# Decode attention plus MLP on one Trainium2 core: the second head's keys loaded in two halves, with a TensorE wait for the first half in round 0

## The chip, the core and the metric

The kernel runs on one core of one Trainium2 chip. The metric is the device time of one execution, in microseconds (us). Three runs of the kernel before the change took 1281.58, 1281.71 and 1282.12 us; their median is 1281.71 us. A difference of 0.2% is 2.6 us.

## The reference, cut to what matters

One token `x` (512 values) passes a layer norm, attends over a cache of 32768 positions in each of 32 heads, is projected and added back, and then passes a second layer norm and a small MLP with a mish activation.

```python
q = (layernorm(x) @ wq).reshape(B, 1, H, 128).transpose(0, 2, 1, 3)      # H = 32
scores = einsum("bhqd,bhkd->bhqk", q, k_cache) * 128 ** -0.5             # 32768 keys per head
o = einsum("bhqk,bhkd->bhqd", softmax(scores), v_cache)
h = x + o.transpose(0, 2, 1, 3).reshape(B, 1, 4096) @ wo
z = layernorm(h) @ w1 + b1
h2 = h + (z * tanh(softplus(z))) @ w2
```

All of it is bfloat16. The two caches are 8 MB per head each, 512 MB (537 million bytes) in all, and each byte is read once: the work is almost wholly the reading of the caches.

## The kernel before, in words

**Memory.** The caches pass through `ring`, six slots of 32 KB per partition (lines 321 to 323 and 354). A head's keys fill two slots: partition p holds the 256 keys 256p to 256p+255, so one partition's share of one head is one run of 64 KB in HBM. Keys of even heads live in slots 0 and 1, those of odd heads in slots 2 and 3, values in slots 4 and 5 (`slot_of`, line 461). `wq` starts in the slots of the values.

**The order of the loads** is one list (`order`, lines 446 to 449), which SyncE walks (lines 536 to 571) and which ends in one DMA queue: `wq`, the keys of head 0, the keys of head 1, the values of head 0, the keys of head 2, the values of head 1, and so on, then the weights of the tail. Before it starts a load, SyncE waits until the place is free (`freed_by`, line 481; for values line 565): the values of head 0 for the last use of `wq`, the keys of head 2 for the last transpose of head 0, the values of head 1 for the last product with the values of head 0. A load raises the semaphore `ready` of its slot. `pieces` (line 427) says which loads are cut: the keys of head 0 in two halves of 128 keys per partition, the values of the last head in six parts; every other one is a single DMA of 128 runs of 64 KB.

**TensorE's program** is a loop that exists once in the code and is run 32 times with the round in a register (`_pe_rounds`, line 170). Its parts lie in the code in this order: entry (with the 128 small products that make the queries, line 621), `top`, `head`, `skip`, `mid`, `tail`, `turn`, `rest`. Round n runs `head(n)`: 32 groups of 8 transposes of 128 keys (line 666), each group copied from PSUM to SBUF by VectorE (line 672) and, three groups later, multiplied by the query (line 642); then VectorE takes the maximum (line 706). At the start of `head` TensorE waits for the keys (`keys_in`, lines 76 to 80): both homes' `ready` semaphores against a value worked out from the round. After that come the softmax steps `soft_a` (line 712, maximum over the partitions), `soft_b` (line 717, spread of that maximum) and the exponential on ScalarE (line 722). In round 0 these are the separate block `turn` (lines 741 to 744), which is run once and jumps back to `top`. In every later round they are interleaved in `rest` (lines 746 to 756) with the 256 products with the values of the head before (`pv`, line 693), split 64, 64 and 128.

Of the kernel before, what the change touches and what calls it, by code (L numbers as in the profile page):

```python
# [291 lines left out]
def bass_sequential_preLN__mha_block_cached__dense_activation_mish__decode_kernel(  # L292
    nc: bass.Bass,
    A_x: bass.AP,
    A_k_cache: bass.AP,
    A_v_cache: bass.AP,
    A_wq: bass.AP,
    A_wo: bass.AP,
    B_x: bass.AP,
    B_w1: bass.AP,  # L300
    B_b1: bass.AP,
    B_w2: bass.AP,
    out: bass.AP,
):
    build_kernel(nc, A_x, A_k_cache, A_v_cache, A_wq, A_wo, B_w1, B_b1, B_w2, out)


def build_kernel(nc, A_x, A_k_cache, A_v_cache, A_wq, A_wo, B_w1, B_b1, B_w2, out):
# [3 lines left out]
    H = HD // Dh  # L312
# [29 lines left out]
    def sb(shape, dt, name):  # L342
        cm = nc.sbuf_tensor(name, shape, dt)
        t = cm.__enter__()
        allocs.append(cm)
        return t.ap()
# [21 lines left out]
    gmax = sb([1, 1], F32, "gmax")  # L368
# [39 lines left out]
    sem = nc.alloc_semaphore  # L408
# [3 lines left out]
    ready = [sem(f"ready{i}") for i in range(NS)]  # L412
# [12 lines left out]
    CUTS = {"k": [TPS], "v": [TPS // 2, TPS, 192, 224, 240]}  # L425

    def pieces(what):
        kind, h = what
        at = CUTS[kind] if what in (("k", 0), ("v", H - 1)) else []
        return list(zip([0] + at, at + [SCOLS]))  # L430

    def cut_at(kind, h, r):
        return r in [r0 for r0, _ in pieces((kind, h))]

    def uncut(what):


        kind, h = what
        for r in CUTS[kind]:
            if not cut_at(kind, h, r) and (h == 0 or cut_at(kind, h - 1, r)):  # L440
                n = 1
                while h + n < H and not cut_at(kind, h + n, r):
                    n += 1
                yield r, n
# [5 lines left out]
    cut_sems = {k: {r: sem(f"cut_{k}_{r}") for r in CUTS[k]} for k in CUTS}  # L450

    s_wl = sem("wl")
    w1_sems = [sem(f"w1_{n}") for n in range(len(W1P))]
    w2_sems = [sem(f"w2_{n}") for n in range(len(W2P))]

# [5 lines left out]
    def slot_of(what):  # L461
        if what in HOMES:
            return HOMES[what]
        if what[0] in ("w1", "w2"):
            return HOMES[WL]
        return V_HOME if what[0] == "v" else what[1] % 2 * HALVES
# [6 lines left out]
    def ready_wait(what):  # L473
        if what == WL:
            return (s_wl, 16)
        return (ready[slot_of(what)], 16 * fills[what])

    def free_name(what):
        return "free" + "_".join(map(str, what))

    def freed_by(what):
        if what == WO:
            return done_with("k", H - 2, 0, SCOLS)
        if what[0] == "k" and what[1] > 1:
            return done_with("k", what[1] - 2, 0, SCOLS)
        if what == ("v", 0):
            return [free_name(WQ)]
        return []

    def tiles_of(what):  # L490
        return ring[:, slot_of(what):slot_of(what) + HALVES, :].rearrange("p s (r d) -> p (s r) d", d=Dh)

    def keys_of(cache, h):
        return cache[0, h, :, :].rearrange("(p r) d -> p r d", r=SCOLS)
# [8 lines left out]
    def done_with(kind, h, r0, r1):  # L503
        if kind == "v":
            return [f"pv{h}_{r1}" if r1 in V_EVENTS else f"pv{h}"]
        return [free_name(("k", h, half)) for half in range(HALVES) if r0 < (half + 1) * TPS and r1 > half * TPS]
# [15 lines left out]
    def program(S):  # L522
# [3 lines left out]
        v = nc.vector  # L526
# [4 lines left out]
        def start(dst, src, s):  # L531
            S.dma(SP, lambda: sp.dma_start(dst, src).then_inc(s, 16))  # L532
# [3 lines left out]
        for what in order:  # L536
            slot = slot_of(what)
            if what == ("k", 1):
                S.stay(SP)
            S.wait(SP, freed_by(what))  # L540
            flat = ring[:, slot, :]
            if what[0] == "wq":
                S.wait(SP, ["b1z"])
                start(b1r[0:FJ, :], B_b1[0:FJ * 128].rearrange("(j p) -> j p", j=FJ), s_b1)
                start(b1r[FJ:FJ + 1, 0:FLAST], B_b1[FJ * 128:F].rearrange("(o p) -> o p", o=1), s_b1)
            elif what[0] == "wo":
                start(flat, A_wo.rearrange("(p j) n -> p (j n)", j=32), ready[slot])
            elif what == WL:
                start(wol_v, A_wo[(H - 1) * Dh:H * Dh, :], s_wl)
            elif what[0] == "w1":  # L550
                k = what[1]
                start(w1_v[:, k, :], B_w1[k * 128:(k + 1) * 128, :], w1_sems[k])
            elif what[0] == "w2":
                n = what[1]
                if n + 1 < len(W2_J):
                    j0, j1 = W2_J[n], W2_J[n + 1]
                    start(w2_v[:, j0:j1, :], B_w2[j0 * 128:j1 * 128, :].rearrange("(j p) n -> p j n", p=128), w2_sems[n])
                else:
                    start(w2_v[0:FLAST, FJ, :], B_w2[FJ * 128:F, :], w2_sems[n])
            else:  # L560
                kind, h = what
                rows = keys_of(A_k_cache if kind == "k" else A_v_cache, h)
                for r0, r1 in pieces(what):
                    if kind == "v" and h:
                        S.wait(SP, done_with(kind, h - 1, r0, r1))
                    start(tiles_of(what)[:, r0:r1, :], rows[:, r0:r1, :], cut_sems[kind][r0] if r0 else ready[slot])

                for r, n in uncut(what) if kind == "v" else [(r, H - 1) for r in CUTS["k"] if h == 2]:
                    S.dma(SP, lambda r=r, n=n: sp.sem_inc(cut_sems[kind][r], 16 * n))
        S.dma(SP, lambda: sp.dma_start(out[0, 0, :].rearrange("(c m) -> c m", c=KC), outr[0:128:32, :]).then_inc(s_out, 16),  # L570
              waits=["fin"])
# [20 lines left out]
        for c in range(2 * KC):  # L592
            cols = xr[0:1, c:D:KC] if c < KC else xr[0:1, (c - KC) * 128:(c - KC + 1) * 128]
            S.step(PE, lambda c=c, cols=cols: t_.matmul(X_REG[:, c:c + 1], cols, identb[0:1, 0:1], start=True, stop=True),
                   name=("xT" if c == 2 * KC - 1 else None), waits=(["identb", (s_x, 16)] if c == 0 else ()))
# [22 lines left out]
        for h in range(H):  # L618
            for kc in range(KC):
# [3 lines left out]
                       name=(["q", free_name(("wq",))] if last else None),  # L623
                       waits=(["xn0", ready_wait(("wq",))] if h == 0 and kc == 0 else ()))
# [90 lines left out]

        def soft_b(h):
            S.step(PE, lambda: t_.matmul(B_REG, onesm[0:1, :], gmax[:, :], start=True, stop=True),  # L717
                   name=f"B{h}", waits=[f"gmax{h}", "consts0"], kind="B")
            S.step(DVE, lambda: v.tensor_scalar_mul(nb[:, :], B_REG, -SC), name=f"nb{h}", waits=[f"B{h}"], kind="nb")  # L719

        def soft_exp(h):
# [19 lines left out]
        def turn():  # L741
            soft_a(0)
            soft_b(0)
            soft_exp(0)

        def rest(i):
            t = i - 1
            soft_c(t)
            pv(t, 0, TPS // 2)
            S.unless_final(PE, "soft_a", lambda: soft_a(i))  # L750
            pv(t, TPS // 2, TPS)
            S.unless_final(PE, "soft_b", lambda: soft_b(i))
            pv(t, TPS, SCOLS)
            oev(t)
            if t < H - 1:
                soft_exp(i)
# [84 lines left out]
    log = {}  # L841
    counted = _Sched(nc, False, events, sems, log)
    program(counted)
    nc.sync.dma_start(ring[:, slot_of(WQ), :], A_wq.rearrange("(p k) n -> p (k n)", k=KC)).then_inc(ready[slot_of(WQ)], 16)
    with nc.Block() as block:
        for eng_name, attr in ((POOL, "gpsimd"), (SP, "sync"), (DVE, "vector"), (ACT, "scalar"), (PE, "tensor")):
            emitter = _Sched(nc, True, events, sems, log, only=eng_name)

            def _run(eng, emitter=emitter):
                program(emitter)  # L850
            getattr(block, attr)(_run)
            assert emitter.cnt == counted.cnt
# [31 lines left out]
```

## Time and profile before

| | |
|---|---|
| median of three runs | 1281.71 us |
| the profiled execution's own time | 1281.4 us |
| its span, first to last instruction | 1279.6 us |
| what lies around the span | 1.8 us |
| bytes moved by DMA | 548.35 MB, mean 429 GB/s |
| TensorE matmuls busy | 1019.0 us (80%) |
| VectorE busy | 716.1 us (56%) |
| ScalarE, GpSimd busy | 20.8 us, 0.8 us |

TensorE's work is counted twice in the profile, as PE (matmuls) and PEld (weight loads, which lie beside the matmuls). "issue" is time in which an engine waited for nothing that the profile shows. SPq is SyncE's queue of DMA issues. The DMA queue named "instruction" carries the engines' own code. Times of the trace count from the first instruction of the span. The columns of the view of stretches are: the stretch, its length, then for each engine the busy time and the number of recorded instructions, the granted TensorE clock, the share of the 16 DMA engines that was busy, and GB/s. Register and branch instructions aren't recorded there. In the DMA views a packet is counted where it starts.

### The profile page before, as it was taken

What the parts mean: (1) busy time and instruction counts of PE and PEld (TensorE: products, weight loads), DVE (VectorE), ACT (ScalarE), POOL (GpSimd) and SP (SyncE); (2) the same over time, 40 slices, a digit from 0 to 9 for tenths busy, and PEclk for the clock granted to TensorE, in tenths of its full rate; (3) what the DMA queues carried; (4) which work ended last, traced back from release to release, by engine and by line L of the source; (5) the groups of instructions that cost most, each with busy time, mean ns of one, the idle gap of its engine ahead of it and who ended that gap; (6) DMA issues with size and microseconds to landing.
All of it is one profiled execution on the core that took longest, in us unless ns stands there. A gap on an engine that the chain in (4) does not pass through costs nothing.

```text
span 1279.6 us, 54437 instructions
## 1 busy us (share of the span) xinstructions
PE 1019.0 (80%) x25044; PEld 992.2 (78%) x25044; DVE 716.1 (56%) x1252; ACT 20.8 (2%) x71; POOL 0.8 (0%) x8
## 2 busy tenths in 40 slices
PE   3699777788777798777797777897777887777987
PEld 3699777788777798777797777897777887777885
DVE  2566654466654566545566544666445666445661
ACT  0000000000000000000000000000000000000000
POOL 0000000000000000000000000000000000000000
PEclk9888777788777788767788776888677887767885
DMA  9979999999999999999999999999999999999998
GB/s 425 420 339 426 445 440 426 426 426 459 426 426 426 449 436 426 426 426 459 426 426 426 453 432 426 426 434 451 426 426 426 457 428 426 426 436 449 426 426 355
DMA packets 12584, 548.35 MB, mean 429 GB/s; under 512 B 1343, under 2 KB 2848, under 8 KB 3616
## 3 DMA queue, kind: packets, MB, share of 16 engines
q1 hardware_dynamic: 12574, 548.22, 99.3%
q8 instruction: 8, 0.13, 0.0%
q10 hardware_dynamic: 2, 0.00, 0.0%
HBM read 548.21 MB, written 0.00 MB: 428 GB/s over the span
## 4 chain that ended last, share of the span: by engine, by line
DMA 55%; DVE 23%; PE 18%; SPq 2%; issue 2%; POOL 0%; POOLq 0%
DMA ring<-in_A_k_cache_dram 54%; DVE ering L672 23%; PE ops L693 9%; PE tps L666 7%; SPq L532 2%; PE sps L642 1%; PE hlp L717 1%; PE hlp L712 1%; DMA ring<-in_B_w_dram 1%; PE hlp L727 0%; PE tps L829 0%; DVE pmax L706 0%; DVE outr L834 0%; DVE gmax L714 0%; SPq L68 0%
## 5 line engine op out<-in xcount | busy, mean ns | idle before, releaser
L666 PE MATMUL tps<-identb,ring 128*128 128x128 bf16 x8192 | 671.1, 233 | 218.4 <-DMA ring<-in_A_k_cache_dram 214.5
L672 DVE COPY ering<-tps 128x1024 bf16<-128x1024 bf16 x1024 | 669.7, 692 | 274.5 <-PE tps L666 274.1
L666 PEld LDWEIGHTS tps<-identb,ring 128*128 x8192 | 524.3, 104 | 221.1 <-issue 221.1
L642 PE MATMUL sps<-qcur,ering 128*128 128x1 bf16 x8192 | 343.9, 164 | 11.3 <-DVE ering L672 6.6
L642 PEld LDWEIGHTS sps<-qcur,ering 128*128 128x128 bf16 x8192 | 309.9, 97 | 14.2 <-DVE ering L672 9.4
L693 PEld LDWEIGHTS ops<-pbuf,ring 128*128 128x128 bf16 x8192 | 226.4, 103 | 15.7 <-issue 12.4
L693 PE MATMUL ops<-pbuf,ring 128*128 128x1 bf16 x8192 | 231.1, 165 | 3.1 <-DMA ring<-in_A_v_cache_dram 2.5
L701 DVE TENSOR_TENSOR oT<-ops,rtotc 128x1 f32 x31 | 5.0, 161 | 107.8 <-PE ops L693 107.8
L714 DVE TENSOR_REDUCE gmax<-hlp 1x1 f32<-1x128 f32 x32 | 8.9, 278 | 63.4 <-PE hlp L712 63.4
L719 DVE TENSOR_SCALAR nbias<-hlp 128x1 f32<-128x1 f32 x32 | 5.1, 158 | 63.5 <-PE hlp L717 63.5
L722 ACT ACTIVATE pbuf<-sps,nbias 128x256 bf16<-128x256 f32 x32 | 15.2, 475 | 1229.4 <-PE ops L693 1171.7
L706 DVE TENSOR_REDUCE pmax<-sps 128x1 f32<-128x256 f32 x32 | 13.6, 425 | 14.3 <-PE sps L642 14.3
L712 PE MATMUL hlp<-ident,pmax 128*1 128x128 f32 x64 | 17.2, 365 | 3.5 <-issue 3.5
L717 PE MATMUL hlp<-gmax,onesmat 1*128 1x1 f32 x64 | 18.5, 356 | 0.4 <-DVE gmax L714 0.4
L717 PEld LDWEIGHTS hlp<-gmax,onesmat 1*128 1x128 f32 x64 | 15.8, 304 | 1.3 <-DVE gmax L714 0.9
L727 PE MATMUL hlp<-esum,onesmat 128*128 128x1 f32 x64 | 12.3, 261 | 5.3 <-issue 2.8
L727 PEld LDWEIGHTS hlp<-esum,onesmat 128*128 128x128 f32 x64 | 9.8, 192 | 7.9 <-issue 7.9
L621 PE MATMUL hlp<-xnT,ring 128*128 128x1 bf16 x128 | 3.5, 165 | 9.1 <-DMA ring<-in_A_wq_dram 9.1
L621 PEld LDWEIGHTS hlp<-xnT,ring 128*128 128x128 bf16 x128 | 3.5, 104 | 9.2 <-issue 9.2
L729 DVE RECIPROCAL rtotc<-hlp 128x1 f32<-128x1 f32 x32 | 5.4, 168 | 4.2 <-PE hlp L727 2.4
L625 DVE CAST qT<-hlp 128x32 bf16<-128x32 f32 x1 | 0.2, 192 | 11.4 <-PE hlp L621 11.4
L722 ACT ACTIVATION_READ_ACCUMULATOR pbuf<-sps,nbias 128x1 f32 x32 | 6.2, 194 | 0.0
(75 smaller groups left out, 37.9 us busy)
## 6 DMA issues: line engine op xcount, KB each, us to landing
ring<-in_A_k_cache_dram SPq DMA_DIRECT2D x2, 4096.0 KB, 26.6
ring<-in_A_v_cache_dram SPq DMA_DIRECT2D x3, 2048.0 KB, 11.3
ring<-in_A_wq_dram SPq DMA_DIRECT2D x1, 4096.0 KB, 12.1
ring<-in_A_wo_dram SPq DMA_DIRECT2D x1, 4096.0 KB, 35.3
ring<-in_B_w_dram SPq DMA_DIRECT2D x4, 344.0 KB, 16.8
ring<-in_A_v_cache_dram SPq DMA_DIRECT2D x1, 1024.0 KB, 14.3
ring<-in_A_v_cache_dram SPq DMA_DIRECT2D x2, 512.0 KB, 15.5
ring<-in_B_w_dram SPq DMA_DIRECT2D x1, 640.0 KB, 16.9
```

The source lines that it names most:

```text
L532: S.dma(SP, lambda: sp.dma_start(dst, src).then_inc(s, 16))
L621: S.step(PE, lambda h=h, kc=kc: t_.matmul(Q_REG[:, h:h + 1], wq_v[:, kc, h * Dh:(h + 1) * Dh], xnT[:, 0, kc:kc + 1], start=(kc == 0), stop ...
L642: S.step(PE, lambda r=r: t_.matmul(S_ps[:, col0 + r:col0 + r + 1], ering[:, bg % NE, r, :], qcur[:, :], start=True, stop=True), name=(name ...
L666: S.step(PE, lambda r=r, at=at: t_.matmul(tb[:, r * 128:(r + 1) * 128], key_tile(S, at), identb[:, :], is_transpose=True, start=True, stop ...
L672: S.step(DVE, lambda: v.tensor_copy(ering[:, bg % NE, :, :].rearrange("p r d -> p (r d)"), tb[:, :]), name=f"ev{bg}", waits=[f"trb{bg}"], ...
L693: S.step(PE, lambda r=r: t_.matmul(o_ps[:, 0:1], vt[:, r, :], pbuf[:, r:r + 1], start=(r == 0), stop=(r == SCOLS - 1)), name=(names or Non ...
L706: S.step(DVE, lambda: v.tensor_reduce(pmax[:, :], S_ps[:, 0:SCOLS], AXX, ALU.max), name=f"pmax{h}", waits=[f"qkh{h}"], kind="pmax")
L712: S.step(PE, lambda: t_.matmul(A_REG, pmax[:, :], ident[:, :], start=True, stop=True), name=f"A{h}", waits=[f"pmax{h}", "ident", f"rcp{h - ...
L714: S.step(DVE, lambda: v.tensor_reduce(gmax[:, :], A_REG, AXX, ALU.max), name=f"gmax{h}", waits=[f"A{h}"], kind="gmax")
L717: S.step(PE, lambda: t_.matmul(B_REG, onesm[0:1, :], gmax[:, :], start=True, stop=True), name=f"B{h}", waits=[f"gmax{h}", "consts0"], kind ...
L722: S.step(ACT, lambda: a.activation(pbuf[:, :], S_ps[:, 0:SCOLS], ACTF.Exp, bias=nb[:, :], scale=SC, accum_out=esum[:, :]), name=f"exp{h}", ...
L727: S.step(PE, lambda: t_.matmul(C_REG, onesm[:, :], esum[:, :], start=True, stop=True), name=f"C{h}", waits=[f"exp{h}"], kind="C")
```

## The change

The keys of head 1 are cut like those of head 0: two DMAs of 128 runs of 32 KB in place of one DMA of 128 runs of 64 KB. The first half raises a semaphore of its own, `s_k1`; the second half raises the `ready` semaphore that the whole load raised before, so the wait at the start of `head(1)` stands as it was. TensorE must also know that the first half has landed: `soft_b(0)` gets a second wait, for `s_k1`, which stands in the block `turn` that only round 0 runs. Nothing else differs.

```diff
     def pieces(what):
         kind, h = what
-        at = CUTS[kind] if what in (("k", 0), ("v", H - 1)) else []
+        at = CUTS[kind] if what in (("k", 0), ("k", 1), ("v", H - 1)) else []
         return list(zip([0] + at, at + [SCOLS]))
...
     s_wl = sem("wl")
+    s_k1 = sem("k1")
...
                 for r0, r1 in pieces(what):
                     if kind == "v" and h:
                         S.wait(SP, done_with(kind, h - 1, r0, r1))
-                    start(tiles_of(what)[:, r0:r1, :], rows[:, r0:r1, :], cut_sems[kind][r0] if r0 else ready[slot])
+                    if what == ("k", 1):
+                        s = ready[slot] if r0 else s_k1
+                    else:
+                        s = cut_sems[kind][r0] if r0 else ready[slot]
+                    start(tiles_of(what)[:, r0:r1, :], rows[:, r0:r1, :], s)
...
         def soft_b(h):
             S.step(PE, lambda: t_.matmul(B_REG, onesm[0:1, :], gmax[:, :], start=True, stop=True),
-                   name=f"B{h}", waits=[f"gmax{h}", "consts0"], kind="B")
+                   name=f"B{h}", waits=[f"gmax{h}", "consts0"] + ([] if h else [(s_k1, 16)]), kind="B")
```

## The prediction, made before the changed kernel was run

> **What bounds the kernel now.** First the page, its slices, queues and chain:
>
> ```profile
> DMA  9979999999999999999999999999999999999998
> ...
> q1 hardware_dynamic: 12574, 548.22, 99.3%
> q8 instruction: 8, 0.13, 0.0%
> ...
> DMA 55%; DVE 23%; PE 18%; SPq 2%; issue 2%; POOL 0%; POOLq 0%
> ```
>
> The DMA engines are busy 99.3% of the span; one slice of 32 us, the third, has a 7. So the time is the bytes at full rate plus whatever DMA stands still. The DMA view of two stretches, 90 to 1270 us and 88 to 98 us (40 slices each), says where that is:
>
> ```profile
> DMA  8999999999999999999999999999999999999999
> DMA packets 9881, 508.23 MB, mean 431 GB/s; under 512 B 1094, under 2 KB 1222, under 8 KB 1689
> ...
> DMA  0069602000000000000000000000000009996000
> ```
>
> From 98 us on there is no hole. In the second line a slice is 0.25 us and a packet counts where it starts: data packets start until 89.25 us, last 2.46 us (below), so the engines run dry by about 91.5; nothing starts until 96.25. About **4.8 us** is the only idle time of the DMA, and the most that any change of this kind can win. The chain of waits from 80 to 100 us says why:
>
> ```profile
> 91.05 0.47 PE ops L693 x14
> 91.51 0.59 issue
> 92.10 3.19 PE ops L693 x114
> 95.29 0.02 issue
> 95.31 0.33 SPq L532
> ```
>
> SyncE issues the values of head 1 at 95.31, when TensorE has used those of head 0 for the last time; 0.95 us later data flows. The hole is TensorE being late in round 1. Why it is late shows in the view of stretches, cut where TensorE stood still:
>
> ```profile
> 24.30:29.40 5.10, 5.10 (x64) 5.10 (x64) 3.17 (x5) 0.00 (x0) 0.00 (x0) 1.00 1.03 443
> 29.40:34.57 5.17, 5.17 (x128) 5.05 (x126) 5.17 (x9) 0.00 (x0) 0.00 (x0) 1.00 1.23 529
> 34.57:36.82 2.25, 0.00 (x0) 0.00 (x0) 0.30 (x1) 0.00 (x0) 0.00 (x0) 1.00 1.09 466
> 36.82:41.86 5.04, 5.04 (x120) 4.90 (x119) 4.61 (x8) 0.00 (x0) 0.00 (x0) 1.00 0.96 416
> 41.86:46.47 4.61, 0.00 (x0) 0.00 (x0) 0.65 (x2) 0.00 (x0) 0.00 (x0) 0.95 1.04 444
> 46.47:53.99 7.52, 7.52 (x123) 7.52 (x124) 4.47 (x7) 0.00 (x0) 0.00 (x0) 0.57 0.96 412
> 53.99:57.80 3.81, 3.13 (x85) 2.95 (x82) 3.36 (x7) 0.00 (x0) 0.00 (x0) 1.00 0.79 344
> 57.80:60.85 3.05, 0.00 (x0) 0.00 (x0) 0.05 (x1) 0.00 (x0) 0.00 (x0) 0.81 1.37 586
> 60.85:63.19 2.34, 1.17 (x5) 0.59 (x5) 0.44 (x2) 0.56 (x2) 0.00 (x0) 0.50 0.84 364
> 63.19:86.18 22.99, 22.57 (x512) 22.40 (x513) 21.05 (x33) 0.00 (x1) 0.00 (x0) 0.93 0.97 417
> 86.18:91.51 5.33, 5.33 (x148) 4.80 (x149) 0.91 (x5) 0.00 (x0) 0.00 (x0) 0.58 0.64 274
> 91.51:92.10 0.59, 0.00 (x1) 0.00 (x0) 0.00 (x0) 0.00 (x0) 0.00 (x0) 0.50 0.00 0
> 92.10:95.31 3.21, 3.18 (x114) 3.09 (x113) 0.00 (x0) 0.00 (x0) 0.00 (x0) 0.50 0.00 0
> ```
>
> Round 0 stands still three times (2.25, 4.61 and 3.05 us), in the middle of a group of transposes or scores, with no engine named. The "instruction" queue moved 8 packets of 16 KB (0.13 MB); asked in slices of 0.1 us from 19.5, 34.25, 43.9, 51.0, 58.2, 65.3 and 89.6 us, each slice has one:
>
> ```profile
> q8 instruction: 1, 0.02, 59.6%
> ...
> q8 instruction: 1, 0.02, 66.2%
> ...
> q8 instruction: 1, 0.02, 66.5%
> ...
> q8 instruction: 1, 0.02, 64.1%
> ...
> q8 instruction: 1, 0.02, 62.1%
> ...
> q8 instruction: 1, 0.02, 62.6%
> ...
> q8 instruction: 1, 0.02, 65.9%
> ```
>
> Four of them are followed 2.45 to 2.6 us later by TensorE going on (34.3 and 36.82; 43.95 and 46.47; 58.25 and 60.85; 89.65 and 92.10). TensorE waits for **its own code**, a block of 16 KB at a time, B to H in this order; between two stalls it ran 239 recorded instructions (x120 and x119), the content of a block, in 5.04 us. After 90 us none is fetched until the tail (the stretch 90 to 1270 has none): the loop then runs from what it holds.
>
> I read a fetch as asked for when TensorE enters the block before. Counting 239 recorded instructions back or forward from the stalls, C was asked for at 29.5, D at 36.82, E at 46.47, F at 53.8 and H at 86.9 (half a microsecond into the products with the values); from asking to the packet's start they took 4.8, 7.1, 4.6, 4.4 and 2.7 us. What they wait for is the traffic on the DMA engines. The same view over 24 to 31 us (keys of head 0) and 36.8 to 44.1 us (keys of head 1):
>
> ```profile
> q1 hardware_dynamic: 96, 3.15, 104.0%
> ...
> q1 hardware_dynamic: 47, 3.08, 97.3%
> ```
>
> Runs are packets: 3.15 MB in 96 are 32 KB each, 3.08 MB in 47 are 64 KB. At the page's 426 GB/s, 26.6 per engine, a packet takes 1.23 or 2.46 us. E and F waited about 2 packets of 64 KB, D about 3, C (two of 32 KB, the first of head 1) about 4.9 us' worth, H for the last one before the queue ran dry.
>
> **The change part by part.**
>
> *Two DMAs for one.* The queue's rows of SyncE:
>
> ```profile
> 1.96 1.39 SPq L532 DMA_DIRECT2D ring<-in_A_k_cache_dram  x3
> 16.59 0.33 SPq L532 DMA_DIRECT2D ring<-in_A_v_cache_dram  x1
> ```
>
> One more issue is 0.46 us (1.39 over 3) at 3.4 us; the next, at 16.59, waits for `wq`. Even if the queue were full and the issue stood for 10 us it would be hidden: the keys of head 1 start to flow about 32 us. Rate: 32 KB runs moved 443 GB/s at 24.30 to 29.40, 64 KB runs 416 at 36.82 to 41.86; edge effects of counting at the start are larger than the difference. I take 0; the bounds are 6% of 19.7 us (8.39 MB at 426), 1.2 us, either way.
>
> *The wait in `soft_b(0)`.* Its first half lands near 44 us (4.19 MB at 426 after head 0, which ends about 34); `turn` comes after 50. Behind it are the spread of the maximum and the jump, but it never holds: about 0.02 us of one instruction, once. If that cover went, each late microsecond would delay round 1 by one.
>
> *Shorter packets ahead of the fetches.* This is the term. Taken as a queue of 2 to 3 packets plus part of one, 32 KB gives a wait of 2.5 to 4.4 us, 3.4 in the middle; with 2.5 from packet to first instruction, 5.9 us a block against 5.0 of execution.
>
> - C: its last packet ahead becomes 32 KB: 1.2 us earlier, entered at 35.6.
> - D: asked at 35.6, entered at 41.5 (was 46.47).
> - E: entered at 47.4 (was 53.8; the half clock from 46.47, granted 0.57, after the long stall goes too).
> - F: asked at 47.4, when the last packets of head 1 and the first 64 KB ones of the values mix, 0 to 1.2 us more: entered at 53.3 to 54.5 (was 60.85).
> - `turn`, 2.34 us: round 1 starts at 55.6 to 56.8 in place of 63.19, **about 7 us earlier**. Its keys have landed by about 53.8 (34.1 plus 19.7), so they don't hold it.
>
> The other end of this unknown is that nothing shortens: round 1 at 63.19.
>
> *What is late next: block H.* Before, H was asked for at 86.9 into an emptying queue, 2.7 us. Asked 7 us earlier, at 79.9, it finds the 64 KB packets of head 2: 4.4 to 7.1 us, so its packet starts at 84.3 to 87.0. From that start to the values of head 1 flowing were 96.25 − 89.65 = 6.6 us (2.45, then 3.21 of products, then 0.95): 90.9 to 93.6. The queue runs dry at 91.5. **Gain: 96.25 less the later of 91.5 and 90.9 to 93.6, 4.8 down to 2.7 us**; three of the four waits under full 64 KB traffic were near 4.5, so I take 4.2.
>
> The Trainium skill, "Runtime: NRT & Kernel Launch", Instruction fetch mechanics, calls the crossing of a 16 KiB block of code "mostly hidden"; by that nothing would move, and the third rival below gets its chance. The 4.61 us stall with a fetch in it disagrees.
>
> The Trainium skill, "DMA: Bandwidth & Descriptors", Queues, rings and completion order, lets an engine drain a packet of 9 to 17 descriptors before it turns to another queue; with 64 KB runs that would be an estimated 22 us or more, and no fetch here waited over 7.1.
>
> **The rivals.**
>
> 1. *The wait is a time, not a number of packets.* For: block B. Its 239 instructions before C (29.5) reach back to about 15.1 us, and its packet started at 19.55: 4.4 us with nothing but 32 KB packets on the engines, no shorter than E and F. Against: D's 7.1 and H's 2.7, which follow the queue. With about 4.5 us kept, only the rounding to the next packet shrinks: C stays at 36.82 and D, E and F take 4.5 + 0.6 + 2.5 = 7.6 us each, so 44.4, 52.0, 59.6: 1.2 us won, and H gives them back, since its packet starts when the queue runs dry, at 89.65, in either case. Time: 0 to 1 us less, 1280.4 to 1281.4 in the profile. **28%.**
> 2. *Slower: the loop outgrows what TensorE keeps.* The wait is one more instruction ahead of `rest`, which moves by one. Now no block is fetched in the loop after H. If one had to be fetched every round, it would cost 7.1 + 2.5 us less what TensorE waits for keys anyway:
>
> ```profile
> PE tps L666 <- DMA ring<-in_A_k_cache_dram: 214.5, 30, 8.8
> ```
>
> 214.5 over 30 is 7.2 us, so up to 2.4 us in each of 30 rounds, some 70 us: 1350. It decides from the point where the loop's last instruction crosses into a ninth block. One instruction of 239 a block makes that unlikely. With lesser losses (the rate bound of 1.2 us, a second fetch on one engine): **6%.**
> 3. *The change doesn't reach the stalls*: they belong to something else that only coincides with the fetches, or fetches go to engines whose queue is as deep in bytes. Nothing moves: 1281.4. **6%.**
>
> **How the numbers follow.** The forecast, 60%, is a gain of 4.2 us: 1281.4 − 4.2 = 1277.2 for the profiled execution; the median of the runs shown is 0.3 above it, so 1277.5. Its own range is a gain of 2.7 to 4.8 (with the rate bound 1.2 to 5.5): 1276.2 to 1280.5. For 8 in 10 the first rival must be in: up to 1281.9. A measurement of this kernel tells about 0.2%, 2.6 us, from no change. Faster by more than that: the forecast's 60%. Within it: the first and third rivals with what the forecast loses to H, 33%. Slower: 7%.
>
> **What would show it.** Right: packets of 32 KB from about 32 to 53 us; the fetch after 36 us started within 4.4 us of its block's entry; stalls of 1 to 2 us in place of 4.61; round 1 begun before 57; a longer stall than 0.59 in the products of round 1 (3 to 5 us); no empty slices between 88 and 98. Wrong: the fetch still 7 us after asking though packets are halved (rival 1); any instruction packet between 100 and 1270 us (rival 2); round 1 early and the hole still there, which would mean that H takes it all.

## The result and the profile after

Twelve runs of the changed kernel have a median of 1281.47 us (1279.07 to 1282.21), twelve of the kernel before, taken beside them, 1281.76 us. The ratio is 0.9992, with a 95% interval from 0.9984 to 1.0001: no change that this measurement can tell. Eleven more runs gave a ratio of 1.0001 (0.9992 to 1.0010).

The median hides something. The changed kernel's times lie in **two heaps**: four of the twelve at 1279.07 to 1279.79, the other eight at 1281.38 to 1282.21, and none between (medians 1279.23 and 1281.92). Of the eleven later runs one, at 1280.80, lies between them. The profiled execution, 1279.37 us with a span of 1277.6 us, is one of the lower heap. So its profile shows the change at its best, and the one of the upper heap has to be taken from another run (below).

The view of stretches of the changed kernel, cut where TensorE stands still (columns as before: the stretch, its length, busy time and count of PE, PEld, DVE, ACT, POOL, granted clock, DMA share, GB/s):

```profile
34.59:35.20 0.61, 0.00 (x1) 0.00 (x0) 0.31 (x1) 0.00 (x0) 0.00 (x0) 1.00 0.37 161
35.20:40.24 5.04, 5.04 (x120) 4.90 (x119) 4.62 (x8) 0.00 (x0) 0.00 (x0) 1.00 1.07 458
40.24:41.84 1.60, 0.00 (x0) 0.00 (x1) 0.65 (x2) 0.00 (x0) 0.00 (x0) 1.00 1.02 430
41.84:48.20 6.36, 6.35 (x121) 6.18 (x121) 4.48 (x7) 0.00 (x0) 0.00 (x0) 0.73 0.97 415
48.20:48.94 0.74, 0.00 (x0) 0.00 (x1) 0.25 (x1) 0.00 (x0) 0.00 (x0) 1.00 1.23 531
48.94:52.92 3.98, 3.30 (x83) 3.04 (x83) 3.12 (x6) 0.00 (x0) 0.00 (x0) 1.00 1.03 445
52.92:56.02 3.10, 0.01 (x1) 0.01 (x2) 0.05 (x1) 0.00 (x0) 0.00 (x0) 1.00 1.35 576
56.02:58.31 2.29, 1.12 (x4) 0.58 (x5) 0.44 (x2) 0.56 (x2) 0.00 (x0) 0.51 0.93 401
58.31:81.73 23.42, 23.06 (x513) 22.89 (x513) 21.04 (x33) 0.00 (x0) 0.00 (x0) 0.90 0.97 420
81.73:87.01 5.28, 5.28 (x148) 4.72 (x148) 0.98 (x5) 0.00 (x0) 0.00 (x0) 0.66 0.98 422
87.01:89.73 2.72, 0.00 (x0) 0.00 (x1) 0.00 (x0) 0.00 (x0) 0.00 (x0) 0.50 0.93 392
89.73:92.96 3.23, 3.20 (x114) 3.12 (x114) 0.00 (x0) 0.00 (x0) 0.00 (x0) 0.50 0.00 0
```

The stalls of round 0 are there, shorter: 0.61 for block C (2.25 before), 1.60 for D (4.61), a new one of 0.74 for E, and F's unchanged at 3.10 (3.05). Round 1 starts at 58.31 in place of 63.19, 4.9 us earlier. And half of that is gone again 30 us later: the stall for block H in the products of round 1 is 2.72 us where it was 0.59. SyncE issues the values of head 1 at 92.96, 2.35 us earlier than before, and the hole in the DMA view of 88 to 98 us (a slice is 0.25 us) is smaller but there:

```profile
DMA  0769660000000000000000099790000000099960
```

Data starts again at 93.75 in place of 96.25. The packets of the keys of head 1 are halved as the change says; over 34 to 52 us the queue's row is

```profile
q1 hardware_dynamic: 262, 8.06, 104.1%
```

262 packets for 8.06 MB, 31 KB each with the few small ones. No instruction packet lies between 99 and 1270 us.

### The profile page after: what moved, and what is told of

Its sections match the earlier page's. It is cut to its first block, busy times and chain, and to the rows that moved or that the text cites. A ratio compares the mean times of both kernels' runs of the same rounds, so it can differ in the third digit from the quotient of the medians.

```text
span 1277.6 us, 54439 instructions
## 1 busy us (share of the span) xinstructions
PE 1014.8 (79%) x25044; PEld 987.4 (77%) x25044; DVE 715.7 (56%) x1252; ACT 20.7 (2%) x71; POOL 0.8 (0%) x8
## 4 chain that ended last, share of the span: by engine, by line
DMA 55%; DVE 23%; PE 18%; SPq 2%; issue 2%; POOL 0%; POOLq 0%
DMA ring<-in_A_k_cache_dram 54%; DVE ering L678 23%; PE ops L699 9%; PE tps L672 7%; SPq L533 2%; PE sps L648 1%; PE hlp L723 1%; PE hlp L718 1%; DMA ring<-in_B_w_dram 1%; PE hlp L733 0%; PE tps L835 0%; DVE pmax L712 0%; DVE outr L840 0%; DVE gmax L720 0%; SPq L68 0%
## 5 line engine op out<-in xcount | busy, mean ns | idle before, releaser
L712 DVE TENSOR_REDUCE pmax<-sps 128x1 f32<-128x256 f32 x32 | 13.6, 425 | 14.3 <-PE sps L648 14.3
L723 PE MATMUL hlp<-gmax,onesmat 1*128 1x1 f32 x64 | 18.5, 356 | 0.4 <-DVE gmax L720 0.4
```

Of the source, the lines that this page charges most:

```text
L712: S.step(DVE, lambda: v.tensor_reduce(pmax[:, :], S_ps[:, 0:SCOLS], AXX, ALU.max), name=f"pmax{h}", waits=[f"qkh{h}"], kind="pmax")
```

## The experiments

Two theories were to be told apart. **Theory A** is the prediction's: a fetch of code waits for two to three data packets, so shorter packets shorten it in proportion. **Theory B** is its first rival: under load a fetch needs a time of its own, whatever the packets' size, and only then waits for the end of a data packet on its DMA engine. The diffs are against the changed kernel, with cuts marked by three dots, unless something else is said.

### The changed kernel again, three times

No edit to the program. The first, with eleven runs:

> The changed kernel once more. The twelve times of it lie in two heaps, near 1279.3 and near 1281.8. Theory B (a fetch of code is ready a set time of about 4.5 us after it is asked for and then waits for the end of a data packet on its engine): the two heaps are one 64 KB packet time, 2.4 us, apart, because block H is fetched at the one or at the next packet end; a run of the upper heap shows the H packet about 2.4 us later than 87.2 us, and the values of head 1 issued at about 95.3 in place of 92.96. Theory A (the wait is two to three packets): round 1 of an upper run starts later already, near 61 to 63 us.

Its median was 1281.60 (1279.55 to 1282.31), the profiled execution 1279.55, of the lower heap again. Two more profiled executions followed:

> The changed kernel a third time, for a profile of the upper heap (two of three runs lie there). By theory B its H packet comes at 89.6 to 89.8, when the queue has run dry, in place of 87.2, whatever the start of round 1; the values of head 1 are issued at 95.2 to 95.6; time 1281.4 to 1282.3. In the lower heap: H at 87.2 to 87.4 and 1279.1 to 1279.8.

> The changed kernel a fourth time, with the same two outcomes as the third: H at 89.6 to 89.8 and 1281.4 to 1282.3, or H at 87.2 to 87.4 and 1279.1 to 1279.8. A run with H at 87.3 and a time over 1281 would speak against theory B.

Both were of the upper heap, 1282.75 and 1282.37 us. The chain of waits of the fourth, from 80 to 100 us, in which the line "issue" of 3.27 us is the stall for block H:

```profile
88.12 0.51 PE hlp L723 x2
88.63 0.46 PE ops L699 x14
89.10 3.27 issue
92.37 3.21 PE ops L699 x114
95.59 0.02 issue
95.60 0.33 SPq L533
```

Its row of the instruction queue from 89.75 to 89.85 us, and that of the first profile of the changed kernel from 87.2 to 87.3:

```profile
q8 instruction: 1, 0.02, 67.1%
q1 hardware_dynamic: 2, 0.00, 1.1%
```

```profile
q1 hardware_dynamic: 3, 0.20, 454.3%
q8 instruction: 1, 0.02, 67.6%
```

In the upper run H's packet starts at 89.8, together with nothing but packets of a few bytes: no 64 KB packet starts any more. In the lower run it starts at 87.2 amid 64 KB packets. The DMA view of 88 to 98 us of the upper run has the hole in full, with data again from 96.5:

```profile
DMA  0006900200000000000000000000000000999090
```

Round 1 of the upper run had started at 60.71, **2.5 us earlier than before the change**, and TensorE came to block H's edge at 89.10 in place of 91.51; it then stood 3.27 us, and the values of head 1 were issued at 95.60, where they were issued at 95.31 before. All of the gain was given back at this one block. In all four profiles the time follows H: 87.2 and 87.3 us, with data again from 93.75 and 94.0, gave 1279.37 and 1279.55; 89.7 and 89.8, with data from 96.25 and 96.5, gave 1282.75 and 1282.37. H's two starts are one 64 KB packet time (2.46 us) apart, and so, roughly, are the heaps. Counted back from the stall as in the prediction, H was asked for at 82.4 and 84.1 us in the lower heap, at 84.5 and 85.4 in the upper; in these four the line between the two packet ends lies near 84.3. The kernel before has its lower heap too, only thinner: of its 63 runs here 7 lie below 1280, of 25 of the changed kernel 6.

Theory A's sign, an upper heap that comes from a later start of round 1, doesn't hold: the starts were 58.31 and 60.67 in the lower heap, 60.85 and 60.71 in the upper. The earliest start comes from a shorter wait for F, but 60.67 too was early enough to meet the packet end at 87.3, and 60.71 was not.

### The wait alone

The keys of head 1 are one load again; TensorE's second wait stays, and SyncE raises its semaphore at the start.

```diff
-        at = CUTS[kind] if what in (("k", 0), ("k", 1), ("v", H - 1)) else []
+        at = CUTS[kind] if what in (("k", 0), ("v", H - 1)) else []
...
         S.dma(SP, lambda: sp.sem_inc(ready[HALVES], 16))
+        S.dma(SP, lambda: sp.sem_inc(s_k1, 16))
...
```

> Keys of head 1 whole again, only the wait in the turn block kept (its semaphore is raised by SyncE at the start). Both theories: as before the change, 1281.7, stalls of about 2.3, 4.6 and 3.1 us in round 0, round 1 from 63.2, the hole of 4.8 us back. A third theory, that the moved code of the rest block matters by itself: anything else, 2 us or more away.

1282.03 us; ratio 1.0004 (0.9995 to 1.0013); round 1 from 63.2 us, values of head 1 issued at 95.59. TensorE's added wait and the shift of `rest` by one instruction cost nothing that can be told. Its stalls were 2.53, 1.60, 2.67 and 4.66 us, so the single stall of 4.61 at block D in the profile before was one draw of several.

### Quarters: runs of 16 KB

The keys of head 1 are four loads; the last raises `ready`, the other three `s_k1`.

```diff
-        at = CUTS[kind] if what in (("k", 0), ("k", 1), ("v", H - 1)) else []
+        at = CUTS[kind] if what in (("k", 0), ("v", H - 1)) else []
+        if what == ("k", 1):
+            at = [64, 128, 192]
...
-                        s = ready[slot] if r0 else s_k1
+                        s = ready[slot] if r0 == 192 else s_k1
...
-  waits=[f"gmax{h}", "consts0"] + ([] if h else [(s_k1, 16)])
+  waits=[f"gmax{h}", "consts0"] + ([] if h else [(s_k1, 48)])
```

> Keys of head 1 in four quarters with runs of 16 KB (0.6 us a packet). Theory A: waits from asking to packet of 2.5 packets of 0.6, under 2.5 us, so no stall at D and E, turn at about 51, round 1 at the landing of its keys, 54 to 55. Theory B: the waits stay at 3.5 to 4.5 us, round 1 from 56.5 to 58; the time 1279 or 1281.7 again, by the packet end that H meets.

1281.83 us (1277.98 to 1282.80); ratio 0.9995 (0.9985 to 1.0004). Round 1 began at 60.9 us, later than theory B's 56.5 to 58. The profiled execution (1282.71) has packets of 14 KB in the mean from 36 to 44 us, and the stalls of round 0 are where they were with halves, and no shorter:

```profile
q1 hardware_dynamic: 239, 3.39, 99.5%
```

```profile
34.23 1.79 issue
...
41.06 1.90 issue
...
48.04 1.58 issue
...
53.60 4.98 issue
```

This is the run that decides against theory A, which had no stall at D and E. Counted as in the prediction, from TensorE's entry of the block before to the start of the packet, the fetches of D and E, which were made amid these keys alone, waited:

| runs of the keys of head 1 | profiles | waits of D and E, us | mean | less half a packet |
|---|---|---|---|---|
| 64 KB | before, wait alone, code moved and keys whole | 7.1, 4.6, 4.3, 5.3, 5.4, 4.6 | 5.2 | 4.0 |
| 32 KB | changed (four), code moved, traffic around H halved (two) | 4.2, 4.7, 5.0, 4.7, 4.6, 4.9, 4.9, 4.8, 5.1, 4.9, 6.1, 4.8, 4.0, 4.7 | 4.8 | 4.2 |
| 16 KB | quarters | 4.4, 4.3 | 4.4 | 4.1 |

Take away half a packet (1.2, 0.6, 0.3 us), the mean wait for a packet's end, and some **4.1 us stay at D and E, whatever the packet**. There the size buys 0.4 us at most each time that it is halved, not half the wait (without the one 7.1 the first row's mean is 4.8, and halving bought nothing). The values are few; that the wait isn't in proportion to the packet is beyond their spread, the 0.4 is not.

The 4.1 us are no constant of every fetch, so theory B isn't shown as it stands either. C, asked for where the keys of head 0 give way to those of head 1, waited 4.8 to 5.1 us with the keys of head 1 whole (three profiles), 2.9 to 3.7 with halves (seven) and 4.3 with quarters (one). So TensorE entered C at 35.4 in the mean of the four profiles of the changed kernel where it was 36.9 with whole keys: some 1.5 us of what the halves won in round 0 was won here. F, asked for where the keys give way to the values, waited 4.4 to 4.6 us in four profiles and 5.7 to 6.6 in seven, without regard to the keys' runs. H waited 4.8 and 3.2 us in the lower heap, 4.3 and 5.3 in the upper. What sets the time of a fetch under load stays open. Nor does any run tell a time of 4.1 us from a fixed number of bytes ahead of the fetch: at 26.6 GB/s per engine, the figure of the prediction, 4.1 us are an estimated 109 KB.

### The load taken away

```diff
-            S.wait(SP, freed_by(what))
+            S.wait(SP, done_with("k", 0, 0, SCOLS) if what == ("k", 1) else freed_by(what))
```

> The keys of head 1 are issued only when the last key of head 0 has been transposed, so blocks D, E and most of F are fetched while no data moves. If the fetch is slow because of the load: D and E come within 2.5 us of being asked for and don't stall round 0, which ends near 51. If it is slow by itself: stalls of 1.5 to 2.5 us at D and E as with halves. Either way about 15 to 19 us slower, since the DMA engines stand still from 34 to 51.

1292.17 us, 10.3 us over the kernel before beside it (1281.89), less than the 15 to 19 expected: the load is issued at 46.4, and data stands still from about 34 till then. Round 0 runs through. The short stall before block C, block C with the first instructions of D, and the rest of `head`, with DMA shares of 0, 0.01 and 0.02:

```profile
34.03:34.29 0.26, 0.01 (x1) 0.00 (x0) 0.26 (x1) 0.00 (x0) 0.00 (x0) 1.00 0.00 0
34.29:39.33 5.04, 5.03 (x125) 4.99 (x125) 4.66 (x9) 0.00 (x0) 0.00 (x0) 1.00 0.01 3
39.33:46.38 7.05, 7.05 (x180) 7.05 (x177) 7.05 (x12) 0.00 (x0) 0.00 (x0) 1.00 0.02 5
```

No gap between 34.29 and 46.38 and the full clock throughout. D's packet started at 36.46, 2.2 us after it was asked for at 34.29, E's at 40.90, some 1.7 us after D was entered (about 39.2, when the 239 recorded instructions of C are through). So a fetch alone takes about 2 us; for D and E the load on the DMA engines adds as much again, plus the packet's end. Which part of the load adds it, none of the runs shows.

### The traffic around H halved too

```diff
+    HALF = [("v", 0), ("k", 2)]
...
+        if what in HALF:
+            at = [TPS]
...
+                        s = s_half[what] if what in HALF else ...
...
+                if what == ("k", 2):
+                    for one in HALF:
+                        S.wait(SP, [(s_half[one], 32)])
+                        S.dma(SP, lambda one=one: sp.sem_inc(ready[slot_of(one)], 16))
```

> As the changed kernel, and the values of head 0 and the keys of head 2 in halves of 32 KB runs too; SyncE waits for both and passes the landing on, so it can't issue the values of head 1 before the keys of head 2 have landed, near 92 us. Theory B: H is asked for at about 82.5 and comes 4.2 to 5 us later, never a 2.4 us step later, so all runs lie in one heap at 1279 or a little under; round 1 still starts at 57 to 58.5. Theory A: H's wait falls to 3 us, its stall to 1 us, the values of head 1 issued at about 92.5 (the landing), 1278.8 to 1279.

1300.40 us, and nothing learnt of H: SyncE's two waits stood ahead of the raising of the cut semaphore without which round 1 can't pass its middle, so round 1 stood until the keys of head 2 had landed at 92 us. (D's wait of 6.1 us, the longest among 32 KB packets, is from this run.) With the waits behind it:

> The same as the run before it with SyncE's pass-on put behind the raising of the cut semaphores that round 1 needs. Theory B (a fetch takes about 4.3 to 6 us from asking under load, whatever the run size, and then the end of a data packet): H asked for at 82 to 84, its packet at 86.5 to 89, in steps of 1.2 us where it was 2.4; the values of head 1 at 92.5 to 95; median between the two heaps, about 1280. Theory A (packets): 1279 in every run.

1280.28 us (1278.41 to 1281.50); ratio 0.9987 (0.9979 to 0.9996). The heaps are gone: the eleven times are spread over 3 us with no gap above 0.8. The profiled execution (1279.16) has H's packet at 87.56, 4.1 us after it was asked for, and the values of head 1 issued at 93.22. So the 64 KB packets around H make the two heaps, as far as eleven runs show it. Their ends would then cost the changed kernel about 1.2 us of its median (1281.47 less 1280.28), but the intervals of the two ratios overlap, so this size isn't shown.

### The code moved

By theory B a fetch isn't made short while data flows; it can only be kept off the path. `mid` and `tail`, which the loop doesn't use before its end, lie between `head` and `turn`; the edit emits `turn` and `rest` directly behind `head`, once with halves and once on the kernel before. The order of the blocks, by name:

```
before:  head, skip, mid, tail, turn, rest, over
here:    head, skip, turn, rest, over, mid, tail
```

> The changed kernel with the code of turn and rest put ahead of mid and tail, so that turn lies in block E, which round 0 holds already: no stall of 3 to 5 us ahead of the softmax of round 0. Round 1 from 54 to 56 (its keys' landing) in place of 58.3 to 60.7; the last block of rest asked for near 80, fetched at 84.8 or 87.2: a gain of 2.4 to 4.8 us in nearly every run, median 1278.5. If blocks don't matter there: 1281.5 as the changed kernel.

> The kernel before with the same move of code and the keys of head 1 whole. Stalls at C and D as before, none ahead of the softmax: round 1 from 59 to 60 in place of 63.2; the last block asked for near 83, fetched at 87.2 or 89.6: lower heap more often, median 1279.5 to 1281. If the halves matter as much as the move, it is 2 us over the kernel with both.

With halves 1278.39 us (1275.70 to 1280.60), ratio 0.9972 (0.9962 to 0.9981); with the keys of head 1 whole 1277.86 us (1275.76 to 1280.07), ratio 0.9976 (0.9966 to 0.9986). The second is better than the 1279.5 to 1281 expected of it. **Both beat the kernel before, by intervals well clear of 1 though the gain is under 0.3%, and the halves add nothing to it**: the intervals lie on each other. The changed kernel was not run beside them; its ratios of 0.9992 and 1.0001 lie above both. The time behind the last data packet is as before (11.0 us with both, 11.1 before), so the gain doesn't come from the tail. The chain of waits of the kernel with halves, from 20 to 100 us:

```profile
53.82 0.44 DVE pmax L712
54.25 0.04 issue
54.30 0.40 PE hlp L718 x2
...
55.05 0.38 PE hlp L723 x2
55.42 0.99 issue
...
84.01 0.81 PE ops L699 x27
84.82 2.44 issue
87.26 2.87 PE ops L699 x101
90.14 0.33 SPq L533
```

After the maximum (L712) there is no stall; it was 3.1 to 4.7 us in the four profiles of the changed kernel. Round 1 starts at 56.41, the last block of `rest` comes at 84.85, the values of head 1 are issued at 90.14, and the DMA view of 86 to 98 us (a slice is 0.3 us) has no hole left, since no run of zeros is as long as a 64 KB packet (2.46 us):

```profile
DMA  0999990009900000699660070009990500099905
```

## Why the prediction was right or wrong, point by point

- **What bounds the kernel**: right. The hole near 92 us is the DMA's only one, and what moved the time of the changed kernel and of those with the code moved was that hole. With the code moved it closes, and the gain is 3.5 to 4 us, under the 4.8 given as the most.
- **Two DMAs, one more wait**: the wait is right at nothing, by the run with the wait alone (1.0004). The second DMA was not run by itself; the pair with the code moved (1278.39 with halves, 1277.86 with whole keys) shows no cost of it beyond their intervals.
- **Shorter packets ahead of the fetches**: this is the step that failed. "Taken as a queue of 2 to 3 packets plus part of one" gave a wait of 3.4 us; at D and E it is 4.8 with 32 KB and 4.4 with 16 KB, where the same step would give under 2.5 us. The rows that spoke against it were on the table: block B's 4.4 us among 32 KB packets stood in the first rival, and was given less weight than D's 7.1, which turned out to be one draw (4.3 in the run with the wait alone). The step's sums came out mixed: C entered at 35.2 to 35.7 (35.6 forecast), D at 41.84 (41.5), E at 48.94 (47.4), F at 56.02 (53.3 to 54.5) in the best profile; in the three others D at 42.6 to 42.9, E at 49.9 to 50.1, F at 58.3 to 58.5. Round 1 was early by 4.9 us at best and 2.4 us more often, not by 7.
- **What is late next**: right in kind. H was named as the place that takes gain away, its stall put at 3 to 5 us (2.72, 1.21, 2.45 and 3.27 in the four profiles), and the 6.6 us from its packet to the first data held (6.5: 87.2 and 93.75). Where it went wrong follows from the step before: with round 1 only 2.4 us early, H is asked for at 84.1 to 85.4, and of three such fetches one met the packet end at 87.3 and two that at 89.7, the same moment as before. That was the first rival's last sentence, "H gives them back".
- **The first rival** (28%) had the outcome: a wait that doesn't shrink with the packets, and H giving the gain back. Its 1280.4 to 1281.4 in the profile, 0.3 more in the median, holds the median of 1281.47. It kept about 4.5 us for the wait, close to the 4.4 to 4.8 of D and E. It left C at 36.82, which came at 35.2 to 35.7, so it put the gain of round 1's start at 1.2 us where 2.4 to 4.9 were measured.
- **The ninth block** and **a change that doesn't reach the stalls** did not happen: no fetch between H and the tail, and the stalls did move.
- The median of 1281.47 lies in the range only through the first rival; the upper end, 1281.9, is 0.2 above what the rivals' sums give (1281.4 and 0.3). The likeliest case, a clear gain, did not come: its mechanism was wrong, and that the range holds is owed to the rival, not to the forecast.

## What to carry to other kernels

Before a wait is put down to the size of what stands ahead of it, look for the same wait under another size: the trace of before had one, and the quarters said the same in one run. A gain in one round is worth what the next wait leaves of it; here the block of code that the earlier round asked for earlier came no earlier in most runs. Where code comes in blocks by DMA while data flows, as here, lay what is run next directly behind what is run now, so that fewer blocks are fetched on the path: moving unused code off the path won 0.24 to 0.28%, where cutting the data's runs won nothing.

## What the runs showed that was not expected

- A fetch of 16 KB of code took about 1.7 to 2.2 us from asking to its packet with the DMA engines idle. With them full it took 4.0 to 5.4 us at D and E (once 6.1, once 7.1), at 64, 32 and 16 KB packets alike, and 2.9 to 6.6 us at C, F and H.
- While data flows its packet starts at the end of a data packet: in the traces of all twelve profiles such an end lies within 0.01 us of it. Block B, which no edit touches, started at 18.2 to 18.5 us in six profiles and at 19.5 to 19.8 in the other six, one 32 KB packet (1.23 us) apart. With 64 KB packets around H this makes two heaps of times some 2.7 us apart in one and the same kernel; with 32 KB there they run together.
- After D's stall of 4.61 us the granted clock was 0.57 over the next 7.5 us, so that a stall can cost more than its length. But after one of 1.60 us it was 0.73 over the next 6.4 in the changed kernel and 1.00 over the next 5.1 in the run with the wait alone: the stall's length doesn't settle it, and no run shows what does.
